# Skip term on TensorE, a third yy buffer, row sums in their own PSUM tile, and a table of the task order

## The chip, the core and the metric

One core of a Trainium2 chip runs the whole program. It has five engines, each with its own queue that runs in order: TensorE (matmul; "PE", with weight loads "PEld"), VectorE ("DVE"), ScalarE ("ACT"), GpSimd ("POOL") and SyncE ("SP", which issues most DMAs). Engines wait for each other through semaphores. The metric is the device time of one execution in microseconds (us). The runs before lie between 969.08 and 975.69 us.

## The reference

One layer with adaptive layer norm: a state-space convolution (S4D) and a gated feed-forward part, on a sequence of 2048 rows of 640 channels.

```python
dt = exp(log_dt); A = -exp(log_A_real) + 1j * A_imag
C = (C_real + 1j * C_imag) * dt[:, None]
P = exp((A * dt[:, None])[:, :, None] * pos)         # 640 x 128 x 2048
K = 2 * einsum("dn,dnl->dl", C, P).real
y = irfft(rfft(u.T, 4096) * rfft(K, 4096), 4096)[:, :2048].T + u * D_skip
mod = silu(c) @ w_mod                                 # sa, ca, ga, sb, cb, gb
x = x + ga * y(layernorm(x) * (1 + ca) + sa)
h = layernorm(x) * (1 + cb) + sb
x = x + gb * ((silu(h @ w1) * (h @ w3)) @ w2)
```

The skip term u * D_skip is the same as D_skip added to the element of K at lag zero.

## The kernel before

The 640 channels run as five blocks (b = 0 to 4) of 128. For each block the kernel does, on a mixture of all engines:

- **Generation** (tasks g{b}.{c}, eight chunks c of 16 channels; function gen_chunk). GpSimd adds up phases (ph) and multiplies exponent tables into sizes (z0 to z2: two into the tile yy, one into xx). ScalarE turns phases into sines and cosines (s0 to s4, PSUM tiles tr). VectorE multiplies sizes and sines (m0 to m4), in place in yy and xx. TensorE multiplies yy and xx (task p, 32 instructions in four column groups) into a PSUM tile kps of 128x256: values of the kernel K. ScalarE copies it to the tile ks (task r), and VectorE adds D_skip (tile dsk) to column 63 of each of the four rows of 64, which is lag zero (task d).
- **Normalised input** (tasks h{b}.{i}): rows of x are loaded (tile xq), normalised by ScalarE or VectorE into a PSUM tile hn (n; four instructions), multiplied and shifted by VectorE (x, a; tile hb), stored to DRAM and fetched in another order into the tile xb.
- **First transform** (hh{b}.{i} of xb and k{b}.{i} of ks): TensorE into PSUM tiles ps, copied by ScalarE or VectorE into sp or sp2.
- **Second transform, product, inverse** (w{b}.{i} and z{b}.{j}): TensorE makes fh and fk, ScalarE copies fh to hz, VectorE multiplies them as complex numbers into fp, TensorE transforms back into fz, and ScalarE or VectorE copies fz to zt, which SP stores to the DRAM tensor zd.

The tables of exponents of a block come from al8{b} (al times 0 to 7), exp{b} (ScalarE) and mag{b}.

After the last block comes a passage: zd is loaded again (iz, and izb for the last block's columns), TensorE makes the last transform (iy, iyb), VectorE adds it to x and takes the statistics of the second layer norm, TensorE turns the rows (tp) and the feed-forward part begins (gu, then groups with X, c and acc). The function ffn and what it calls run to the end.

The order up to the start of the feed-forward groups is not written out by hand. Every piece of work is a task with an engine (or a choice of two, as ("ACT", "DVE")), a duration that the code supposes, the tasks before it, and the buffers that it takes and gives back (rings: ph, xx, yy two each, kg two halves of kps, tr three, and so on). The planner, Plan.place, plays these durations through: it starts ready tasks by the rank of each, for which a list RANKS holds one number per task, and picks the engine that ends first where there is a choice. The kernel then emits the instructions in that order. As every engine runs its queue in order, this order decides what waits.

Most instructions go through one helper, so that all of them carry its line (157); the tiles tell them apart.

Of the kernel before, what the change touches and what calls it, by code (L numbers as in the profile page):

```python
# [29 lines left out]
EXPS = ((0, 0, 0, 64.0), (0, 1, 0, 1.0), (1, 0, 0, 512.0), (1, 1, 4, 8.0), (1, 2, 0, 8.0))  # L30
# [3 lines left out]
RANKS = """  # L34
# [65 lines left out]
"""  # L100
FP = 2
EPS = 1e-5
MAGIC = 1.5 * 2.0 ** 23
REV = float(2 ** 32 - 256)
# [63 lines left out]
class Plan:  # L168
# [101 lines left out]
    def run(self):  # L270
# [6 lines left out]
        for s, f, e, n in self.order:  # L277
            if T[n][2]:
                T[n][2](e)
# [1896 lines left out]
```

## Time and profile before

| | us |
|---|---|
| median of 3 runs | 973.34 |
| lowest, highest | 969.08, 975.69 |
| the profiled execution | 972.31 |
| its span, first to last instruction | 970.5 |
| TensorE busy in it | 859.9 |
| VectorE busy | 702.0 |
| ScalarE busy | 546.4 |
| GpSimd busy | 340.5 |

The time of an execution is a little longer than its span, by 1.8 us in the profiled one. Busy time is a sum over the whole span, in which the engine that limits changes, so shares of the whole say little; the stretches tell more. TensorE's granted clock was 0.975 of full speed over the span. In rows of the profile a group is named by tile written <- tiles read, without buffer numbers; the times of a group are its busy total, the mean of one instruction, and the idle time of its engine just before them with what ended it. Matmuls that the program issues once show as two records.

### The profile page before, as it was taken

The page shows a single profiled execution, that of the slowest core. Times are in us where ns is not written, and L with a number is a line of the kernel's source. Part 1 is how long each engine was busy: PE and PEld are TensorE (multiplying, and loading weights), DVE is VectorE, ACT ScalarE, POOL GpSimd, SP SyncE. Part 2 cuts the span into 40 slices and gives each one's busy share as a digit, 9 for nine tenths or more (in the row PEclk, how much of TensorE's full clock was granted, in tenths as well). Part 3 has the DMA queues.
Part 4 walks back from the last instruction along what each step waited for, and adds up shares of the span by engine and source line. Part 5 has one row for each costly group of instructions (what it writes and reads, how often), then busy time and mean ns, then how long its engine had stood idle before and what let it go on. Part 6 is the DMA issues. An engine that isn't in the chain of part 4 may idle for free.

```text
span 970.5 us, 20551 instructions
## 1 busy us (share of the span) xinstructions
PE 859.9 (89%) x7985; PEld 681.8 (70%) x7985; DVE 702.0 (72%) x1395; ACT 546.4 (56%) x1022; POOL 340.5 (35%) x371
## 2 busy tenths in 40 slices
PE   1464787889899997899999999999999999999997
PEld 1132665767778884677777778888788888888775
DVE  7998899999999968886767677557456464645422
ACT  6877788979888851564434455346444344443412
POOL 1797889879799600002111111000011212120000
PEclk9996999999999999799999999999999999999999
DMA  9955453723425268935434422276342322220374
GB/s 218 275 168 191 111 136 95 177 66 106 111 80 152 74 159 206 241 118 182 122 120 139 122 96 68 82 209 194 112 134 64 102 77 86 82 82 28 108 220 133
DMA packets 110506, 127.31 MB, mean 131 GB/s; under 512 B 10568, under 2 KB 90696, under 8 KB 109128
## 3 DMA queue, kind: packets, MB, share of 16 engines
q1 hardware_dynamic: 109032, 125.21, 45.3%
q8 instruction: 63, 1.03, 0.5%
q10 hardware_dynamic: 1376, 0.79, 0.3%
q14 instruction: 35, 0.29, 0.1%
HBM read 95.82 MB, written 30.15 MB: 130 GB/s over the span
## 4 chain that ended last, share of the span: by engine, by line
PE 70%; DVE 17%; ACT 5%; issue 4%; DMA 3%; POOL 1%; SPq 1%; ACTq 0%; DVEq 0%
PE c L157 19%; PE acc L157 18%; PE X L157 12%; PE ps L157 4%; PE gu L157 3%; DVE yy L157 3%; PE kps L157 3%; PE fz L157 2%; PE fk L157 2%; DVE fp L157 2%; PE fh L157 2%; DVE hn L157 2%; DVE xx L157 2%; DVE xb L157 1%; ACT tr L157 1%
## 5 line engine op out<-in xcount | busy, mean ns | idle before, releaser
L157 PE MATMUL acc<-ah,w 128*128 128x512 f32 x560 | 173.2, 395 | 2.4 <-DMA w<-w2d 1.7
L157 PEld LDWEIGHTS acc<-ah,w 128*128 128x128 f32 x560 | 103.7, 188 | 26.4 <-issue 2.1
L157 PE MATMUL acc<-al,w 128*128 128x512 f32 x260 | 102.4, 394 | 0.0
L665 DVE TENSOR_TENSOR wl<-s,wh 128x256 fp32r<-128x256 f32 x92 | 38.9, 423 | 67.5 <-ACT wh L664 67.1
L841 POOL TENSOR_TENSOR s<-wr 128x256 f32<-128x256 f32 x22 | 16.4, 744 | 187.8 <-DMA wr<-in_w 94.8
L157 POOL TENSOR_TENSOR ph<-p,p 128x1024 int32<-128x1024 int32 x40 | 79.2, 1979 | 8.2 <-ACT tr L157 8.0
L664 ACT ACTIVATE wh<-s 128x256 fp32r<-128x256 f32 x92 | 37.6, 410 | 78.5 <-PE X L157 58.1
L157 PE MATMUL kps<-yy,xx 128*32 128x64 f32 x2560 | 51.8, 234 | 28.6 <-DVE xx L157 21.4
L157 DVE TENSOR_TENSOR yy<-yy,tr 128x512 f32<-128x512 f32 (+1 forms) x80 | 75.3, 943 | 1.2 <-ACT tr L157 0.6
L157 PEld LDWEIGHTS kps<-yy,xx 128*32 128x32 f32 x2560 | 45.1, 116 | 38.3 <-issue 22.0
L664 ACT ACTIVATE wh<-wr 128x256 fp32r<-128x256 f32 x92 | 38.4, 418 | 56.0 <-PE X L157 42.3
L842 POOL TENSOR_TENSOR s<-s,wr 128x256 f32<-128x256 f32 x22 | 16.6, 755 | 134.0 <-issue 133.9
L902 ACT ACTIVATE t<-g 128x512 f32<-128x512 f32 x44 | 27.8, 632 | 52.7 <-DVE g L866 52.7
L157 ACT ACTIVATE tr<-ph,hpi 128x512 f32<-128x512 f32 x80 | 54.6, 690 | 4.4 <-DVE xx L157 2.7
L157 PEld LDWEIGHTS acc<-al,w 128*128 128x128 f32 x260 | 48.9, 188 | 10.8 <-DVE al L665 0.3
L871 DVE SCALAR_TENSOR_TENSOR g<-t,g 128x512 f32<-128x512 f32 x48 | 33.7, 702 | 31.3 <-ACT t L902 29.3
L157 POOL TENSOR_TENSOR yy<-e,e 128x512 f32<-128x512 f32 x48 | 52.4, 1109 | 8.8 <-PE kps L157 5.9
L157 DVE TENSOR_TENSOR xx<-tr,xx 128x512 f32<-128x512 f32 x80 | 54.3, 680 | 1.1 <-ACT tr L157 1.1
L157 PE MATMUL ps<-wk,ks 128*64 128x128 f32 x640 | 42.4, 285 | 13.6 <-DVE ks L157 8.9
L157 ACT ACTIVATE tr<-ph 128x512 f32<-128x512 int32 x80 | 47.3, 598 | 12.4 <-DVE yy L157 6.5
L157 PE MATMUL ps<-wk,xb 128*64 128x128 f32 x640 | 46.1, 295 | 6.3 <-ACT sp L157 3.0
L157 PEld LDWEIGHTS ps<-wk,ks 128*64 128x64 f32 x640 | 37.0, 143 | 20.3 <-ACT hn L157 6.6
(448 smaller groups left out, 2379.7 us busy)
## 6 DMA issues: line engine op xcount, KB each, us to landing
w<-w2d SPq DMA_DIRECT2D x42, 640.0 KB, 3.9
wr<-in_w SPq DMA_DIRECT2D x50, 320.0 KB, 3.9
zd<-zt SPq DMA_DIRECT2D x40, 256.0 KB, 2.9
w2d<-w SPq DMA_DIRECT2D x14, 640.0 KB, 3.5
xs<-in_x SPq DMA_DIRECT2D x16, 320.0 KB, 11.3
hs<-hb SPq DMA_DIRECT2D x20, 256.0 KB, 2.5
xb<-hs SPq DMA_DIRECT2D x20, 256.0 KB, 4.9
iz<-zd SPq DMA_DIRECT2D x32, 160.0 KB, 5.0
```

What stands on the lines that cost most here:

```text
L157: self.prev = self.k.order(f(*a, **kw), self.prev)
L664: self.nc.scalar.activation(H, v, AF.Copy)
L665: eng.tensor_tensor(Lo, v, H.bitcast(F32), op=ALU.subtract)
L841: eng.tensor_tensor(s[0], u[:, 0:2], u[:, 2:4], op=ALU.add)
L842: eng.tensor_tensor(s[1], s[0], g[:, 0:2], op=ALU.subtract)
L871: V.scalar_tensor_tensor(g, th, 1.0, g, op0=ALU.add, op1=ALU.mult)
L902: tanh = lambda o, i: A.activation(o, i, AF.Tanh, scale=0.5)
```

## The change

Five things change, all in the part ahead of the feed-forward groups.

1. The skip term. The task d on VectorE is gone. Behind the 32 products of a chunk, TensorE adds D_skip into column 63 by four products of 32x32 with four columns (identity times dsk), on the four diagonal corners of the array.
2. Ten of the 40 chunks (every third one of the first four blocks) keep yy in memory that belongs to the tile x2[0], which is needed only later: a third buffer (ring yz).
3. kps is a tile of its own per chunk, with one buffer (ring kg has one instead of two halves). ScalarE's copy r gives it back.
4. The order. Plan.place and its numbers are gone; ORDER lists the index of every task in the order in which it is emitted, and a mark ' where the second engine of a choice is taken. Nothing is played through any more.
5. What the order stands on: al8 is made in the tile of the table itself, so that it needs no tile of its own (the exponents are then taken with the one that overwrites it last); the products x0 and x1 are one task; the first two tiles of iz lie in sp2 and so can be loaded before the generation buffers are closed; fh and fk have another order of their four parts. The code for other forms of the product (FORM) is there but every block uses the same as before.

The supposed durations of many tasks change as well, but nothing reads them now.

```diff
-        self.plan = plan = Plan(ph=2, xx=2, yy=2, tr=3, kg=2, f2=3, bank=4, hz=3, xq=2, fp=FP, zt=3, xs=4, st=1, gu=3, tmp=7, w2=3)
+        self.plan = plan = Plan(ph=2, xx=2, yy=2, yz=1, tr=3, kg=1, f2=3, bank=4, hz=3, xq=2, fp=FP, zt=3, xs=4, st=1, gu=3, tmp=7, w2=3)
...
-RANKS = """
--1152 -1540 -1534 -1515 -1509 -1417 -1345 -1436 -1412 -1402 -1385 -1330 -1273 -1351 -1452 -1478 -1480 -1475 -1459 -1510 -1507
+ORDER = """
+1 78 80 81 82 83 150' 84 2 19 20 21 22 23 14 15 41 42 43 24 25 16 44 45 46 47 26 17 27 48 36 49 18 50 4 37 5 51 96 33 30 28 100 98
...
-EXPS = ((0, 0, 0, 64.0), (0, 1, 0, 1.0), (1, 0, 0, 512.0), (1, 1, 4, 8.0), (1, 2, 0, 8.0))
+EXPS = ((0, 0, 0, 64.0), (1, 0, 0, 512.0), (1, 1, 4, 8.0), (1, 2, 0, 8.0), (0, 1, 0, 1.0))
...
+    def in_third(self, b, c):
+        return b < NB - 1 and (8 * b + c) % 3 == 2
+
+    def third(self):
+        return self.x2[0].rearrange("p j d -> p (j d)")[:, :2048].rearrange("p (r d a i) -> p r d a i", r=2, d=self.CD, a=2)
...
-        yy = w.tile([P, 2, C, 2, 32], F32, name=f"yy_{d0}", tag="yy")
+        yy = self.third() if self.in_third(d0 // P, d0 % P // C) else w.tile([P, 2, C, 2, 32], F32, name=f"yy_{d0}", tag="yy")
...
+            for q in range(4):
+                g = slice(32 * q, 32 * q + 32)
+                nc.tensor.matmul(kps.rearrange("p (e b) -> p e b", b=64)[g, :, 63], self.ident[g, g], self.dsk[g, d0 // P, d0 % P // 4:d0 % P // 4 + 4],
+                                 start=False, stop=True, skip_group_check=True, tile_position=(32 * q, 32 * q))
...
-                if b == c == 0:
-                    self.kg = self.psg.tile([P, 2, 256], F32, name="kps", tag="kg", bufs=1)
-                kps[c] = self.kg[:, c % 2]
+                kps[c] = self.psg.tile([P, 256], F32, name=f"kps{b}{c}", tag="kg", bufs=1)
...
-        def skip(c):
-            o = slice(4 * c, 4 * c + 4)
-            V.tensor_add(self.ks[b][:, o, 63], kps.pop(c).rearrange("p (e b) -> p e b", b=64)[:, :, 63], self.dsk[:, b, o])
...
-            add(n + "d", "DVE", .1, lambda c=c: skip(c), [n + "r"] + (["dsk"] if b == 0 else []), t + 3, give=[("kg", n + "p")])
...
-        four = lambda x: x.rearrange("p (q r d) -> p q r d", q=2, r=2)
+        four = lambda x: x.rearrange("p (r q d) -> p q r d", q=2, r=2)
...
-            if u < 3:
-                z[u] = [self.ip.tile([P, 2, 512], F32, name=f"iz{u}{pr}", tag=f"iz{pr}", bufs=3) for pr in range(2)]
-            else:
-                z[u] = [self.xb[:, 1024 * pr:1024 * pr + 1024].rearrange("p (a d) -> p a d", a=2) for pr in range(2)]
+            s = self.sp2.rearrange("p a b c -> p (a b c)")
+            t = s[:, :2048] if u == 0 else s[:, 2048:] if u == 1 else self.xb if u == 3 else self.ip.tile([P, 2048], F32, name="iz2")
+            z[u] = [t[:, 1024 * pr:1024 * pr + 1024].rearrange("p (a d) -> p a d", a=2) for pr in range(2)]
...
+    def sequence(self):
...
+        for x in ORDER.split():
+            n = names[int(x.rstrip("'"))]
...
+            out.append((engs[x.endswith("'")], n))
```

Three places show how the instructions move. The first is VectorE's queue in the second block, at the chunks that start with channels 224 and 240 (the number behind tr); ks<-kps,dsk is the skip addition, hn<-xq the normalising. Before:

```order
L157 TENSOR_TENSOR yy_1627<-yy_1627,tr_224_1848 128x1024
L157 TENSOR_TENSOR ks_1194<-kps,dsk 128x4
L157 TENSOR_SCALAR hn<-xq_1590,rs_y_h,rs_n_h 128x128 x4
L157 TENSOR_TENSOR fp_1828<-fk_1859,hz_1854 128x2x2x128
L157 TENSOR_TENSOR xx_1626<-tr_224_1868,xx_1626 128x512
L157 TENSOR_TENSOR fk_1859<-fk_1859,hz_1854 128x512
L157 TENSOR_TENSOR hn<-hn,rw 128x512
L157 TENSOR_TENSOR fp_1828<-fp_1828,fk_1859 128x256 x2
L157 TENSOR_TENSOR hb_1958<-hn,rw 128x512
L157 TENSOR_TENSOR ks_1194<-kps,dsk 128x4
L157 TENSOR_SCALAR hn<-xq_1703,rs_y_h,rs_n_h 128x128 x4
L157 TENSOR_TENSOR xx_1697<-tr_240_1870,xx_1697 128x512
```

The same chunks after the change, where x_94 is the third yy buffer:

```order
L151 TENSOR_TENSOR xx_1721<-tr_224_1820,xx_1721 128x512
L151 TENSOR_TENSOR hn<-hn,rw 128x512
L151 TENSOR_TENSOR hb_1894<-hn,rw 128x512
L151 TENSOR_TENSOR x_94<-x_94,tr_224_1919 128x1024
L151 SCALAR_TENSOR_TENSOR yy_1853<-yy_1853,tr_240_1923 128x16x32
L151 TENSOR_TENSOR yy_1853<-yy_1853,tr_240_1923 128x16x32
L151 TENSOR_TENSOR xx_1721<-tr_224_1938,xx_1721 128x512
L151 COPY sp<-ps_1979 128x64x8
L151 TENSOR_TENSOR hn<-hn,rw 128x512
L151 TENSOR_TENSOR hb_1995<-hn,rw 128x512
L151 COPY sp_1013<-ps_2006 128x64x8
L151 COPY sp<-ps_2015 128x64x8
```

The skip additions are gone and the normalising has left VectorE (over the kernel 20 of these instructions stay on it instead of 44), while copies of ps have come to it (27 instead of 20).

The second place is TensorE's queue at the first second-transform groups (fh, fk) of block 0, between two chunks of generation. Before:

```order
L157 MATMUL kps<-yy_1091,xx_1090 32x64 x32
L157 MATMUL fh_1341<-sp,wb 64x128 x8
L157 MATMUL fk_1354<-sp,wb 64x128 x8
L157 MATMUL fh_1372<-sp,wb 64x128 x8
L157 MATMUL fk_1392<-sp,wb 64x128 x8
L157 MATMUL kps<-yy_1171,xx_1170 32x64 x32
```

After:

```order
L151 MATMUL kps_1342<-yy_1137,xx_1136 32x64 x32
L151 MATMUL kps_1342<-dsk,ident 32x4 x4
L151 MATMUL fh_1395<-sp,wb 64x128 x8
L151 MATMUL fh_1412<-sp,wb 64x128 x8
L151 MATMUL fk_1433<-sp,wb 64x128 x8
L151 MATMUL fk_1456<-sp,wb 64x128 x8
L151 MATMUL kps_1465<-yy_1191,xx_1190 32x64 x32
L151 MATMUL kps_1465<-dsk,ident 32x4 x4
```

Each chunk has four skip products behind its own 32; between two chunks other groups stand as before.

The third place is SP's queue at the end of the last block: xb<-zd loads the fourth inverse tile, zd<-zt stores a result of the last block, izb<-zd loads its columns. Before:

```order
L157 DMA xb<-zd 64x2x512 x4
L157 DMA zd<-zt_5189 128x4x128
L157 DMA zd<-zt_5191 128x4x128
L157 DMA zd<-zt_5208 128x4x128
L157 DMA zd<-zt_5210 128x4x128
L157 DMA izb_5243<-zd 64x4x128 x2
```

After:

```order
L151 DMA xb<-zd 64x2x512 x2
L151 DMA zd<-zt_5316 128x4x128
L151 DMA zd<-zt_5332 128x4x128
L151 DMA zd<-zt_5337 128x4x128
L151 DMA xb<-zd 64x2x512 x2
L151 DMA izb_5402<-zd 64x4x128 x2
```

Two of the four loads of the inverse tile have moved behind the last stores.

More of the change, by code (lines that the diff above doesn't have):

```diff
@@ L168 @@
 class Plan:
-    LAG = dict(PE=0.2, DVE=0.18, ACT=0.2, POOL=0.15, SP=0.0)
-    CHAIN = dict(DVE=0.12, ACT=0.12, POOL=0.07)
-    NEAR, RATE, LAND, FLY, ISSUE, AWAY, TABLE = 0.1, 235e3, 1.3, 0.7, 0.06, 8, 1.28
     def __init__(self, **rings):
@@ L258, in place @@
+        taken, done, out = {r: [] for r in self.n}, set(), []
+        for x in ORDER.split():
+            n = names[int(x.rstrip("'"))]
+            engs, _, _, after, _, _, take, give, _, _ = T[n]
+            assert n not in done and done.issuperset(after), n
+            for r, y, _ in take:
+                i = len(taken[r]) - self.n[r]
+                assert i < 0 or not uses[r, taken[r][i]], n
+                taken[r].append(y)
             for k in give:
                 uses[k] -= 1
-                given[k] = max(fin + self.LAG.get(e, 0.0), given.get(k, 0.0))
@@ L261, in place @@
[L261 to L279 removed]
+            done.add(n)
@@ L282 @@
+            out.append((engs[x.endswith("'")], n))
+        assert len(done) == len(T)
+        return out
+    def run(self):
+        for e, n in self.sequence():
+            if self.tasks[n][2]:
+                self.tasks[n][2](e)
 class K:
@@ L1113, in dst @@
                         return z[u][pr][h * 64:h * 64 + 64]
-                    load(f"iz{u}.{pr}{h}", zv[:, t0:t0 + 2, :cut], dst, 262144, done + ([f"hh{b4}.{i}.m" for i in range(8)] if u > 2 else []))
+                    load(f"iz{u}.{pr}{h}", zv[:, t0:t0 + 2, :cut], dst, 262144, done + ([f"hh{b4}.{i}.m" for i in range(8)] if u > 2 else []),
+                         "inv" if u < 2 else "change")
         def load_up(m):
@@ L1135, in load_down @@
                      [f"w2l{0 if m == 1 else 13}"] if m in (1, 2) else [])
[L1137 removed]
+        used = [f"g{b4 - 1}.{c}.z{i}" for c in (5, 6, 7) for i in range(3)] + [f"mag{b4 - 1}", f"exp{b4 - 1}"]
         for b, src in ((0, b4 - 1), (1, b4)):
@@ L1613, in border @@
             self.x2 += [self.fp.tile([P, 4, D], F32, name=f"x2{i}") for i in (2, 3)]
-        plan.add("change", None, 0, change, [f"g{b}.7.p", f"g{b}.7.d"] + [f"h{b}.{i}.x" for i in range(4)], 0, own=True)
+        plan.add("change", None, 0, change, [f"g{b}.7.p", f"g{b}.7.r"] + [f"h{b}.{i}.x" for i in range(4)], 0, own=True)
         self.tail_tasks(border, cut)
```

269 lines of the change are left out of this document (117 added, 152 removed), and 87 rows, old and new, of tables (ORDER, RANKS).

## The prediction

> **What bounds the kernel now.** I first cut the span into stretches of busy time, at the points where the chain of waits changes its character. The columns are the stretch, its length, busy time (and instructions) of TensorE, its weight loads, VectorE, ScalarE and GpSimd, then the granted clock, the DMA share and GB/s.
>
> ```profile
> core 0: us, PE busy (x) PEld busy (x) DVE busy (x) ACT busy (x) POOL busy (x), PEclk, DMA share, GB/s
> 0.00:100.00 100.00, 41.52 (x633) 23.90 (x633) 87.83 (x171) 75.12 (x143) 66.43 (x80) 0.90 0.74 210
> 100.00:252.00 152.00, 124.75 (x2464) 103.80 (x2464) 145.42 (x275) 128.95 (x217) 132.20 (x132) 0.96 0.49 124
> 252.00:376.00 124.00, 118.93 (x2312) 98.26 (x2314) 109.62 (x208) 86.49 (x156) 75.45 (x72) 1.00 0.44 116
> 376.00:398.00 22.00, 13.92 (x79) 8.87 (x76) 19.45 (x76) 6.47 (x10) 0.63 (x1) 0.72 0.91 215
> 398.00:441.00 43.00, 41.00 (x184) 32.75 (x183) 35.78 (x68) 25.78 (x46) 0.91 (x1) 0.99 0.59 176
> 441.00:971.00 530.00, 519.77 (x2319) 414.21 (x2317) 303.95 (x601) 223.60 (x453) 64.91 (x87) 1.00 0.38 115
> ```
>
> From 441 us on TensorE is busy 519.77 of 530 us, in code that the change leaves alone. Whatever the change does must be done before that. There VectorE is the full engine from 100 to 252 us (145.42 of 152), and TensorE from 252 to 376 us (118.93 of 124). The chain of waits says the same; its columns are start, length, engine, tile and line:
>
> ```profile
> 251.81 0.61 DVE xx L157
> 252.55 0.87 PE kps L157 x41
> ...
> 373.19 2.01 PE fz L157 x8
> ...
> 376.30 3.14 DMA zd<-zt
> ...
> 380.31 4.67 DMA izb<-zd
> ...
> 398.07 8.88 PE gu L157 x36
> ```
>
> Up to 252 us the chain runs mostly over VectorE pieces, then over TensorE up to the last inverse product at 373 us, then over two transfers into the first feed-forward product at 398 us. So the sum has three parts: VectorE's work before 252 us, TensorE's work from 252 to 376 us, and the passage to 398 us.
>
> **The change part by part.** These groups carry the prices (busy total and mean ns behind the first bar, idle time before them behind the second):
>
> ```profile
> L157 DVE TENSOR_TENSOR ks<-kps,dsk 128x4 f32<-128x4 f32 x40 | 6.0, 157 | 9.8 <-ACT ks L157 5.6 <-PE kps L157 3.1 <-ACT hn L157 1.1
> L157 DVE TENSOR_SCALAR hn<-xq,rs_y_h,rs_n_h 128x128 f32<-128x128 f32 x44 | 18.1, 412 | 1.2
> L157 DVE COPY sp<-ps 128x512 f32<-128x512 f32 x20 | 13.4, 683 | 3.2 <-PE ps L157 3.1
> L157 DVE TENSOR_TENSOR xs_al<-al,j 128x1024 f32<-128x1024 f32 x1 | 2.8, 2835 | 0.0
> L157 DVE TENSOR_TENSOR late<-late,mag 128x512 f32<-128x512 f32 x1 | 1.7, 1718 | 0.0
> L157 DVE TENSOR_SCALAR p<-pB 128x128 int32<-128x128 int32 x4 | 1.9, 481 | 0.0
> L157 ACT ACTIVATE hn<-xq,rs_n_h,rs_y_h 128x128 f32<-128x128 f32 x20 | 9.2, 462 | 2.5 <-DMA xq<-in_x 1.7 <-DVE fp L157 0.3
> L157 ACT ACT_TABLE_LOAD x12 | 15.4, 1283 | 1.3 <-PEq L2172 0.7 <-DVE xx L157 0.4
> L157 ACT ACTIVATE sp<-ps 128x512 f32<-128x512 f32 x60 | 35.3, 595 | 11.0 <-PE ps L157 10.0 <-DMA xs_w<-in_w_mod 0.7
> ```
>
> *The skip additions on VectorE go.* All 40 of 157 ns go; by the stretches 24 of them, 3.58 us, lie before 252 us:
>
> ```profile
> 0.00:100.00 100.00, 0.79 (x5) 0.30 (x1) 0.90 0.74 210
> 100.00:252.00 152.00, 2.79 (x19) 0.00 (x0) 0.96 0.49 124
> ```
>
> They also held VectorE's queue for 9.8 us, because each waited in order for ScalarE's copy of its chunk. Of that the list of VectorE's waits from 252 us on has 5.8 us, where VectorE doesn't bind:
>
> ```profile
> DVE ks L157 <- ACT ks L157: 5.0, 4, 2.8
> ...
> DVE ks L157 <- PE kps L157: 0.8, 1, 0.8
> ```
>
> That leaves 4.0 us before 252 us. Part of it comes back at the next instruction, which may be no readier: between 0 and 4.0 I take 2.0.
>
> *The order moves work off VectorE.* Counted over the two programs, 24 of the 44 normalising instructions go to ScalarE (24 x 412 ns = 9.9 us); the exponent and magnitude products of the second block, done beside busy GpSimd, go to GpSimd (2.84 + 1.72); two p copies go too (2 x 481 = 0.96). The hn row stands the same in the list for 100 to 252 us alone, and the two products stand in the chain before:
>
> ```profile
> 88.58 2.76 DVE xs_al L157
> ...
> 98.62 1.72 DVE late L157
> ```
>
> Seven more copies of sp come to VectorE (683 ns each), of which the first three blocks have a net three: +2.0 us.
>
> Before 252 us: -3.6 - 2.0 - 9.9 - 4.6 - 1.0 + 2.0 = **-19.1 us**.
>
> Is there cover for it on the others? TensorE has 124.75 us of work in 152, and keeps its skip products (below, 18 chunks x 0.3 = 5.4): 130.2 us in a stretch that by VectorE shrinks by some 12 to 140, a load of 93%, where it reached 96% from 252 us on. GpSimd gets two products more, in the first 100 us where it idles 33.6. ScalarE is the narrow one: see the second rival.
>
> *The skip products on TensorE come.* Four 32x32 products with four columns per chunk, so 40 x 4 instructions. No row shows one. Nearest below is the chunk's own product, 32 instructions in 64 records, 1.10 us; nearest above the four small products of the modulation, 8 records in a row, 1.05 us:
>
> ```profile
> 317.36 0.91 PE fh L157 x16
> 318.27 1.10 PE kps L157 x61
> ...
> 321.29 1.06 PE fk L157 x16
> ...
> 103.50 1.05 PE L157 MATMUL pv<-ident,mc 128*128 128x4 f32 x8
> 252.00:376.00 124.00, 18.47 (x960) 15.79 (x960) 2.45 (x16) 6.11 (x16) 1.00 0.44 116
> ```
>
> At 1.10/64 a record, 8 records are 0.14 us; serial they would be 1.05. A group that follows one of another shape also shows 1.06 where the same sixteen take 0.91: 0.15 for the change of shape. I take 0.14 + 0.15 = 0.3 us, near the lower end since the four lie in four corners of the array as the chunk's own do. From 252 us on 960/64 = 15 chunks pay it on the engine that binds: **+4.5 us** (+2.1 to +15.8). Before that it is covered as shown above. The Trainium skill, TensorEngine Tiling (Array Packing), section Instruction Overhead, says that a product of one column takes as long as one of 60; this would set each of the four at the price of the chunk's own 64-column products, and the sum by it would be 2.1 instead of 4.5, the lower end.
>
> *Third yy buffer, single kps tile.* GpSimd waited 14.9 us for the two yy buffers:
>
> ```profile
> POOL yy L157 <- PE kps L157: 14.9, 11, 3.9
> ```
>
> GpSimd isn't on the chain there, so I count nothing for it. The row sums now have one PSUM tile where two halves rotated: the next chunk's product waits in TensorE's queue until ScalarE has copied the last one, and everything behind it waits too. In the new order at least one other group of 0.9 us or more stands between two chunks, which covers a copy of 0.38 us (15.06 us over 40); if ScalarE is late the wait shows. Zero, with the rivals for more.
>
> *The passage.* On SP the last two loads of the fourth inverse tile now stand behind the stores of the last block, in front of the loads of the last columns:
>
> ```profile
> iz<-zd SPq DMA_DIRECT2D x32, 160.0 KB, 5.0
> 386.61 0.69 DVE L157 TENSOR_TENSOR x<-iyb,x 128x512 f32<-128x512 f32 x1 [1.33 <-PE iyb L157]
> ```
>
> Issued near 376.7 us, where the store's piece of the chain starts, they land some 5 us later; two row products, two additions of 0.69 us and statistics stand before the addition that now starts at 386.61. I estimate 387.4 in its place: **+0.8 us** (0 to 1.5). The feed-forward part gets the same instructions: 0.
>
> Sum: -19.1 + 4.5 + 0.8 = -13.8 us. The profiled run was 972.31 us (span 970.5), so 958.5 there; the median of the runs, 973.34, lies 1.0 above it: **960 us** rounded up. Own range: waits 2.0 either way, skip products -2.4 to +4, passage 0.8: 953 to 967.
>
> **The rivals.**
>
> *ScalarE takes over (964 to 972, say 966).* From 100 to 252 us ScalarE has 128.95 us of work; 24 x 462 ns and one table load come, two copies of 595 go: 128.95 + 11.1 + 1.3 - 1.2 = 140.2 us, which is the whole 140 that VectorE would leave. At VectorE's present density of 145.42/152 it needs 146.5, so 6.5 of the gain goes: -7.3 in all. Against it: ScalarE idles 24.9 us in the first 100 and 37.5 from 252 us on, and an order can move work there.
>
> *The four products run one after another (980).* This is the slower end. At 1.05 us a chunk, 15 chunks cost 15.8 in the bound stretch, and before it TensorE has 124.75 + 18.9 = 143.7 us, at 96% density 149.6 instead of 140: -13.8 + 11.3 + 9.6 = +7, 979.4 for the profiled run. It decides from about 0.8 us a chunk. For it: the pv row. Against: the chunk's own products overlap. It is also what a rule would do: the Trainium skill, TensorEngine Tiling (Array Packing), section Restrictions and Gotchas, says that different row tiles cannot use the same PSUM bank at once, and these four are row tiles with one target tile; no row before shows row tiles on one bank.
>
> *The order packs better (948).* All 4.0 us of waits go, the skip products cost 2.1, and the 6.6 us that VectorE idles between 100 and 252 us go to work: 958.5 - 2.0 - 2.4 - 6.6 + 1 = 948.5. For it: GpSimd runs ahead with the third buffer. Against: every engine is over 80% there.
>
> **How the numbers follow.** Forecast 0.57, ScalarE 0.22, serial products 0.10, better packing 0.11. Less than about 1% (963.6 to 983.1 around 973.34) can't be told from no change. Faster: 0.57 x 0.85 + 0.22 x 0.2 + 0.11 = 0.64. Same: 0.57 x 0.15 + 0.22 x 0.8 = 0.26. Slower: the serial case, 0.10, counted whole although its 980 lies just inside 1%, since the price leaves out what queues behind TensorE. The range 947 to 975 holds the first, second and fourth case.
>
> **What would show it.** The additions ks<-kps,dsk are gone; VectorE's busy total up to the last inverse product falls by some 17 us; hn on ScalarE stands at 44 and TensorE is under 97% before the handover. Chunk groups of kps rise from 1.10 to some 1.4 us: 2 or more proves the serial rival. The last fz should start near 360 instead of 373, and the first gu near 385. ScalarE at 95% or more before the handover, with VectorE waiting for tr, would make the second rival right. Waits of kps for ScalarE's ks would show the single tile, which I count as free.

## The result, and the profile after

| | before | after |
|---|---|---|
| median of 11 runs each, us | 974.80 | 968.31 |
| lowest to highest | 969.08 to 976.63 | 965.61 to 969.84 |
| ratio, 95% interval | | 0.9944, 0.9926 to 0.9962 |
| the profiled execution, its span | 972.31, 970.5 | 969.31, 967.5 |
| VectorE, ScalarE busy in it | 702.0, 546.4 | 697.6, 554.9 |

The change gains 5.4 us by the ratio (3.7 to 7.2 by its interval), where 13 were forecast. The direction is right, and more than half of the gain is missing: 968.3 lies above the forecast's own range of 953 to 967, and inside 947 to 975 only because that takes the rivals in.

The same stretches as before, with the same columns (stretch, length, busy time of TensorE, its weight loads, VectorE, ScalarE, GpSimd, then granted clock, DMA share, GB/s), of the changed kernel:

```profile
0.00:100.00 100.00, 37.16 (x532) 21.07 (x533) 87.46 (x166) 73.92 (x139) 63.18 (x80) 0.88 0.77 204
100.00:252.00 152.00, 132.07 (x2835) 111.84 (x2825) 137.96 (x232) 137.41 (x241) 133.53 (x132) 0.96 0.42 113
252.00:376.00 124.00, 118.27 (x2388) 96.17 (x2386) 110.01 (x193) 88.16 (x155) 78.15 (x75) 1.00 0.50 131
376.00:398.00 22.00, 15.10 (x79) 9.65 (x76) 19.75 (x69) 5.34 (x9) 0.63 (x1) 0.77 1.04 245
```

From 100 to 252 us VectorE fell from 145.42 to 137.96 and ScalarE rose from 128.95 to 137.41: two engines at 90% where one stood at 96%. Most of what VectorE no longer does there did not become time; VectorE idles instead. The groups say on whom it waits (busy total and mean ns, then the idle time before them and what ended it):

```profile
L151 DVE TENSOR_TENSOR xx<-tr,xx 128x512 f32<-128x512 f32 x80 | 54.4, 683 | 8.1 <-ACT tr L151 7.8
L151 DVE TENSOR_SCALAR hn<-xq,rs_y_h,rs_n_h 128x128 f32<-128x128 f32 x20 | 8.2, 412 | 0.8 <-ACT zt L151 0.2
L151 DVE COPY sp<-ps 128x512 f32<-128x512 f32 x27 | 18.0, 683 | 1.3 <-PE ps L151 1.2
L151 ACT ACTIVATE hn<-xq,rs_n_h,rs_y_h 128x128 f32<-128x128 f32 x44 | 20.4, 464 | 1.1
L151 PE MATMUL kps<-dsk,ident 32*32 32x4 f32 x320 | 9.8, 181 | 0.0
```

In the kernel before, the first of these waited 1.1 us for ScalarE's tr; now 7.8. Where the stages stand, in us from the start of the span:

| | before | after | difference |
|---|---|---|---|
| ScalarE's copy of the last chunk's row sums | 346.44 | 344.48 | -2.0 |
| first fh of the last block | 349.87 | 346.14 | -3.7 |
| last fz | 373.19 | 371.57 | -1.6 |
| first gu | 397.73 | 396.13 | -1.6 |
| end of the span | 970.5 | 967.5 | -3.0 |

This execution was a late one: four of the experiments below (e2, e7, e13, e15) have the same instructions up to the last chunk, and copied its sums at 341.6 to 342.2. Measured by those, some 4.5 us are gained there, against the one profile of the kernel before, which is 2.5 us below that kernel's median; so this is good to some 2 us. About 1 is lost on the way to gu (51.3 us from that copy before, 52.3 in e13), and 1.4 come behind it (572.8 us from gu to the end, then 571.4).

The loss in the last block has one place. TensorE's rows (start, length, group, idle time before it and what ended it), and the pieces of the chain that lead there:

```profile
361.58 1.08 PE L151 MATMUL fh<-sp,wb 128*64 128x128 f32 x16
365.30 1.14 PE L151 MATMUL fh<-sp,wb 128*64 128x128 f32 x16 [2.63 <-ACT zt L151]
```

```profile
342.56 6.06 DMA sp<-zd
...
351.04 7.46 DMA sp<-zd
...
360.09 4.45 DMA zd<-zt
...
364.64 0.61 ACT zt L151
```

sp<-zd are loads of the first two tiles of iz, which lie in sp2; the new order puts them ahead of the stores on SP. SP waited for two of them to land; the store zd<-zt therefore went out at 360.09, its buffer came free at 364.5, ScalarE copied into it, and TensorE had idled 2.63 us.

### The profile page after: what moved, and what is told of

The parts are those of the page before. It is cut to its first block, busy times and chain, and to the rows that moved or that the text cites. A ratio compares the mean times of both kernels' runs of the same rounds, so it can differ in the third digit from the quotient of the medians.

```text
span 967.5 us, 21165 instructions
## 1 busy us (share of the span) xinstructions
PE 861.4 (89%) x8305; PEld 684.7 (71%) x8305; DVE 697.6 (72%) x1334; ACT 554.9 (57%) x1041; POOL 342.1 (35%) x375
## 3 DMA queue, kind: packets, MB, share of 16 engines
q8 instruction: 65, 1.06, 0.5%
## 4 chain that ended last, share of the span: by engine, by line
PE 66%; DVE 8%; ACT 6%; DMA 4%; issue 3%; SPq 1%; POOL 0%; DVEq 0%; ACTq 0%
PE c L151 19%; PE acc L151 18%; PE X L151 12%; PE ps L151 3%; PE gu L151 3%; PE kps L151 2%; PE fh L151 2%; PE fz L151 2%; PE fk L151 2%; DMA sp<-zd 1%; PE iy L151 1%; DVE fp L151 1%; DVE yy L151 1%; ACT tr L151 1%; DVE hn L151 1%
## 5 line engine op out<-in xcount | busy, mean ns | idle before, releaser
L151 DVE TENSOR_TENSOR yy<-yy,tr 128x512 f32<-128x512 f32 (+1 forms) x60 | 56.7, 946 | 4.5 <-ACT tr L151 2.8
L805 DVE SCALAR_TENSOR_TENSOR g<-t,g 128x512 f32<-128x512 f32 x48 | 33.7, 702 | 31.5 <-ACT t L836 29.6
L599 DVE TENSOR_TENSOR wl<-wr,wh 128x256 fp32r<-128x256 f32 x92 | 40.3, 438 | 15.0 <-ACT wh L598 14.9
L151 PE MATMUL kps<-yy,xx 128*32 128x64 f32 x1920 | 38.2, 234 | 14.1 <-DVE xx L151 11.5
L151 PEld LDWEIGHTS kps<-yy,xx 128*32 128x32 f32 x1920 | 33.5, 116 | 23.2 <-issue 13.0
L151 PE MATMUL fz<-fp,wz 64*128 64x512 f32 x160 | 43.0, 627 | 5.9 <-DVE fp L151 4.6
```

The source lines that it names most:

```text
L151: self.prev = self.k.order(f(*a, **kw), self.prev)
L599: eng.tensor_tensor(Lo, v, H.bitcast(F32), op=ALU.subtract)
L805: V.scalar_tensor_tensor(g, th, 1.0, g, op0=ALU.add, op1=ALU.mult)
```

## The experiments

Each was run in five rounds beside the kernel before on the same chip; ratios are to that. A difference from the changed kernel is worked out from the ratio, 0.001 being 0.97 us; with intervals of about 0.0015 to 0.0025 either way, under 2 us can't be told from none. "Last chunk" is ScalarE's copy of the last chunk's row sums. In the table of the order a number is a task, a mark ' the second engine of its choice.

### One part undone, or done alone

**e1: the normalising back on VectorE**, at the same places.

```diff
-554 564 817 827 1080 1085
+554' 564' 817' 827' 1080' 1085'
```

> The changed kernel, with the 24 normalising instructions of the second to fourth block back on VectorE at the same places of the order. Theory A (ScalarE became as full as VectorE between 100 and 252 us, 137.4 and 138.0 us busy, so the 9.9 us that VectorE lost were not a gain): VectorE goes to about 148 us and ScalarE to about 126 there, the time stays within 2 us of the changed kernel's 968.3. Rival B (VectorE is the bound as the forecast counted it, and what is missing of the gain was lost elsewhere): the 9.9 us come back in full, about 978.

Ratio 1.0022 (1.0005 to 1.0038): 7.6 us worse than the changed kernel, nearer to rival B. Read beside the next run, it is not the worth of the move.

**e5: the same 24 instructions to ScalarE, in the kernel before**, nothing else.

```diff
         for s, f, e, n in self.order:
             if T[n][2]:
-                T[n][2](e)
+                T[n][2]("ACT" if n in ("h1.0.n", "h1.2.n", "h2.1.n", "h2.3.n", "h3.2.n", "h3.3.n") else e)
```

> The kernel before, in its own order, with the same 24 normalising instructions on ScalarE that the change moves there, and nothing else. Theory A (the forecast's term: VectorE is the bound between 100 and 252 us and ScalarE has room): 9.9 us less than before, a ratio of 0.990. Rival B (what putting them back in the changed kernel cost, 7.6 us, is their worth): 0.992. Rival C (ScalarE has no room in an order made without them, and the chunks wait for its sines): no gain, 0.997 to 1.003.

Ratio 1.0060 (1.0048 to 1.0072): 5.8 us *slower*. VectorE's waits between 90 and 200 us (engine and tile that waited, on whom; total, times, longest):

```profile
DVE hn L157 <- ACT hn L157: 10.4, 4, 4.5
DVE sp L157 <- PE ps L157: 3.0, 1, 3.0
DVE hn L157 <- ACT sp L157: 2.6, 1, 2.6
```

Before, the first of these stood at 0.6. VectorE's next step multiplies hn, so what it no longer computes it waits for, behind whatever stands in ScalarE's queue. Both orders lose 6 to 8 us when these six tasks change engine and nothing else does, whichever way they go. So neither run gives a worth of the instructions that holds without the order. None of the three theories held in full; A fell.

**e4: the skip term alone, in the kernel before.** The four products go behind each chunk as in the change, and the additions are taken out:

```diff
-            V.tensor_add(self.ks[b][:, o, 63], kps.pop(c).rearrange("p (e b) -> p e b", b=64)[:, :, 63], self.dsk[:, b, o])
+            kps.pop(c)
```

> The kernel before, in its own order, with only the skip term moved: VectorE's 40 additions are gone and TensorE has the four products behind each chunk. Theory A (the step's own terms with the measured 0.17 us: 3.6 us of additions and 2.0 of waits less on VectorE, 2.6 more on TensorE): 3.0 us less than before, 971.8. Rival B (with the forecast's 0.3 us): 1.1 less, 973.7. Rival C (the waits of the additions come back in full at the next instruction and the additions were slack): 1 to 3 more, 975.8 to 977.8.

Ratio 0.9999 (0.9978 to 1.0020). A's 3.0 less is outside the interval (2.1 less to 2.0 more), B's 1.1 less and the lower end of C inside. The skip term's move alone is worth nothing that can be measured, although VectorE's busy time up to the last chunk fell by 4.4 us (319.6 to 315.2).

**e3: the changed kernel without the skip products.**

```diff
-            for q in range(4):
-                g = slice(32 * q, 32 * q + 32)
-                nc.tensor.matmul(kps.rearrange("p (e b) -> p e b", b=64)[g, :, 63], self.ident[g, g], ...
```

> The changed kernel without the four skip products of each chunk: D_skip is left out of the result. Theory A (a group costs the 0.17 us that its start to the next start shows, on the 15 chunks of the stretch where TensorE binds): 2.6 us less, 965.7. Rival B (0.3 us as the forecast had it, with the change of shape): 4.5 us less, 963.8. Rival C (TensorE no longer binds before the feed-forward part, other engines do): under 1 us, 967.5 to 968.3.

Ratio 0.9931 (0.9905 to 0.9956), 1.3 us less. Rival B's 4.5 lies just outside what the two intervals allow (1.3 +- 3); A and C can't be told apart. The rows of the changed kernel give the price of one group directly:

```profile
330.11 0.24 PE L151 MATMUL kps<-dsk,ident 32*32 32x4 f32 x8
330.28 1.13 PE L151 MATMUL fz<-fp,wz 64*128 64x512 f32 x4
```

From its start to the next group's start are 0.17 us, for four products; 33 of the 40 groups show the same.

**e6: the exponent and magnitude products of the second block back on VectorE.**

```diff
-408 410
+408' 410'
```

> The changed kernel, with the exponent and the magnitude product of the second block back on VectorE, as before. Theory A (the forecast's term: 4.6 us of VectorE's time were saved and were worth as much): 4.6 us more than the changed kernel, a ratio to before of 0.999. Rival B (VectorE has as much busy time in the first 100 us as before, 87.5 against 87.8 us, because its small instructions there grew longer beside GpSimd, 0.7 to 2.7 us for h_nm, 0.7 to 2.4 for the first magnitude product; the term was paid back): within 1.5 us of the changed kernel, 0.993 to 0.996.

Ratio 0.9952 (0.9938 to 0.9965), 0.8 us more: the 4.6 of the term are not there. But B's mechanism fell with it. In e6 the two products take 2.07 and 0.95 us, and the small instructions stay as long as in the changed kernel. Those of the changed kernel, and in the second fence GpSimd beside them:

```profile
35.55 2.43 DVE L151 TENSOR_TENSOR e<-e,mag 128x512 f32<-128x512 f32 x1
37.90 1.91 DVE L151 TENSOR_SCALAR h_nm<-h_nm 128x4 f32<-128x4 f32 x1
```

```profile
35.15 4.63 POOL L151 TENSOR_TENSOR ph<-p,p 128x1024 int32<-128x1024 int32 x2
```

An instruction on 128x4 elements took 1.91 us: it ended at 39.81, when GpSimd's second ph ended (39.78). In the kernel before, the same two took 0.68 and 0.16 us, at 31.5 to 32.3, in a gap of GpSimd's. So the new order, not the move of the two products, put them beside it. The Trainium skill, SBUF — State Buffer, section "SBUF: two separate sides", says that VectorE (in a two-port mode, or reading two inputs from SBUF) and GpSimd take a shared pair of ports for a whole instruction, and that the other waits it out. The first row, with two inputs, agrees in its length; for the second, with one input, the trace shows only the wait until GpSimd's end, not which of these conditions it meets.

**e8: two halves for the row sums.**

```diff
-                kps[c] = self.psg.tile([P, 256], F32, name=f"kps{b}{c}", tag="kg", bufs=1)
+                if b == c == 0:
+                    self.kg = self.psg.tile([P, 2, 256], F32, name="kps", tag="kg", bufs=1)
+                kps[c] = self.kg[:, c % 2]
```

> The changed kernel, with the row sums of a chunk in two halves of one PSUM tile again, taken in turn; the order stays. Theory A (the forecast: the single tile costs nothing, since other groups cover ScalarE's copy): within 1 us of the changed kernel, a ratio to before of 0.9935 to 0.9955. Rival B (TensorE waits for the copy of ks and what is queued behind it waits too): 2 to 3 us less, 0.991 to 0.9925.

Ratio 0.9950 (0.9935 to 0.9965), 0.6 us more, that is none. A holds: the single tile costs nothing that can be measured.

### What a microsecond costs on either engine

e1 and e5 change what waits for what. So work was added that nothing waits for: 24 instructions of a constant 128x128 tile into a spare one, behind the six normalising groups (VectorE's form, shown here, in e9 and e11; ScalarE's in e10 and e14).

```diff
-        c.tile([P, 32], F32, name="pad")
+        self.dummy = c.tile([P, P], F32, name="spare")
...
+        if (pc, b) in ((1, 0), (1, 2), (2, 1), (2, 3), (3, 2), (3, 3)):
+            for j in range(4):
+                self.nc.vector.tensor_scalar(self.dummy, self.ident, rstd[:, 0:1], nb[:, 0:1], op0=ALU.mult, op1=ALU.add)
```

e9, in the changed kernel, on VectorE:

> The changed kernel with 24 additional instructions on VectorE that nothing waits for, of the form of the normalising ones (a constant 128x128 tile into a spare tile), at the places in the order of the six normalising groups that went to ScalarE: about 24 x 0.44 = 10.6 us more of VectorE's time and no other change. Theory A (VectorE still sets the pace between 100 and 252 us, as the forecast assumed for its gain): 9 to 10.6 us more, a ratio to before of 1.0035 to 1.0055. Theory B (VectorE, 90.8% busy there, now waits for ScalarE and TensorE and has room for a part): 4 to 7 more, 0.9985 to 1.0015. Rival C (ScalarE alone is the bound): under 2 more, below 0.9965.

e10, in the changed kernel, on ScalarE:

> The changed kernel with 24 additional instructions on ScalarE that nothing waits for, of the form of the normalising ones, at the same six places: about 24 x 0.46 = 11.1 us more of ScalarE's time and no other change. If ScalarE sets the pace together with VectorE (90.4% busy between 100 and 252 us, theory B): 6 to 11 us more, a ratio to before of 1.0005 to 1.0055. If VectorE alone sets it (theory A): under 3 more, below 0.9975.

e11 and e14, in the kernel before, on VectorE and on ScalarE:

> The kernel before, in its own order, with the same 24 additional instructions on VectorE behind its own. Theory A (VectorE is the bound there, 95.7% busy between 100 and 252 us, so a microsecond of its work is a microsecond of the kernel): 9 to 10.6 us more, a ratio of 1.009 to 1.011. Rival (VectorE's neighbours bind as well, and it has room): under 6, below 1.006.

> The kernel before, in its own order, with the 24 additional instructions of e10 on ScalarE. Read at the copy of the last chunk's row sums, since the feed-forward part is longer by the spare tile. Theory A (ScalarE has room in the order before, so it became a second bound by the change): of the 11.8 us added under 5 show there, where VectorE's 16.5 in e11 showed as 17.3. Theory B (in the order before, too, ScalarE's sines are waited for): 8 to 11 show.

The ratios are 1.0161, 1.0158, 1.0254 and 1.0168, with intervals of 0.002 to 0.003 either way, far above every ratio expected. Of each, 8 to 9 us stand behind the first gu, where none of these instructions is, and e13 is for that: only the spare tile.

```diff
-        c.tile([P, 32], F32, name="pad")
+        c.tile([P, P], F32, name="pad")
```

> The changed kernel with nothing but an unused tile of the first pool widened from 32 to 128 columns, as the spare tile of e9 to e11 did, which moves the later tiles of on-chip memory by 384 bytes. Theory A (the 8 us that e9 to e11 show behind the first feed-forward product, 579.5 to 581.0 against 571.4 us, come from where the tiles lie): 8 us more than the changed kernel, all behind gu; the copy of the last chunk's row sums stays near 344.5 us; a ratio to before of 1.002 to 1.0035. Rival (the additional instructions did it): as the changed kernel, 0.993 to 0.996.

Ratio 1.0046 (1.0030 to 1.0061). Theory A holds: the last chunk is copied at 342.02, as ever, and from gu to the end pass 580.1 us instead of 571.4. So e9 and e10 are read against e13, and e11 and e14 at the last chunk. The added instructions took, in e9, e10, e11 and e14 in turn:

```profile
L151 DVE TENSOR_SCALAR spare<-ident,rs_y_h,rs_n_h 128x128 f32<-128x128 f32 x24 | 14.4, 599 | 0.7
```

```profile
L151 ACT ACTIVATE spare<-ident,rs_n_h,rs_y_h 128x128 f32<-128x128 f32 x24 | 11.8, 490 | 0.6
```

```profile
L157 DVE TENSOR_SCALAR spare<-ident,rs_y_h,rs_n_h 128x128 f32<-128x128 f32 x24 | 16.5, 689 | 0.7
```

```profile
L157 ACT ACTIVATE spare<-ident,rs_n_h,rs_y_h 128x128 f32<-128x128 f32 x24 | 11.8, 493 | 0.6
```

| | added, us | cost, us | per us |
|---|---|---|---|
| after, VectorE (e9 less e13) | 14.4 | 11.2 | 0.78 |
| after, ScalarE (e10 less e13) | 11.8 | 10.9 | 0.92 |
| before, VectorE (e11, last chunk 363.92 less 346.44) | 16.5 | 17.5 | 1.06 |
| before, ScalarE (e14, last chunk 355.28 less 346.44) | 11.8 | 8.8 | 0.75 |

A profiled execution is good to some 2 us and the intervals to 3, so these prices are good to some 0.2; read at the last chunk too, e9 and e10 give 0.86 and 1.07. By them e9 is nearer to theory A, e11 has its theory A (and more than its 9 to 10.6 us), and e10 and e14 have their theories B: at these six places work added to VectorE or to ScalarE sets the pace, in both kernels. A microsecond given to ScalarE costs nearly as much as one on VectorE, and in the kernel before already 0.75. The profile before showed ScalarE 85% busy from 100 to 252 us, and the forecast had read that as room. No such price was measured for TensorE.

Does taking away work with the same prices? In e17 and e18 each of the six groups is one instruction of 128x512 instead of four, on ScalarE in the changed kernel, on VectorE in the one before.

```diff
+            if (pc, b) in ((1, 0), (1, 2), (2, 1), (2, 3), (3, 2), (3, 3)):
+                if j == 0 and e == "DVE":
+                    self.nc.vector.tensor_scalar(out, x, rstd[:, s], nb[:, s], op0=ALU.mult, op1=ALU.add)
+                elif j == 0:
+                    self.nc.scalar.activation(out, x, AF.Identity, scale=rstd[:, s], bias=nb[:, s])
-            if e == "DVE":
+            elif e == "DVE":
```

> The changed kernel; each of the six normalising groups that went to ScalarE is one instruction of 128x512 instead of four of 128x128, which takes the mean and scale of the group's first rows for all of them, so that part of the normalisation is left out of the result. ScalarE has 24 x 0.464 - 6 x 0.60 = 7.5 us less, and nothing else changes. Theory B (what ScalarE got counts on the path, 10.2 of 11.8 us in e10): 5 to 6.5 us less than the changed kernel at the last chunk and in all, a ratio to before of 0.988 to 0.9895. Rival A (VectorE alone sets the pace and e10's cost was one of a longer queue only): under 2, 0.9925 to 0.9945.

> The kernel before; the same six groups, on VectorE there, each as one instruction of 128x512 with the first rows' mean and scale, so that part of the normalisation is left out of the result. VectorE has 24 x 0.44 - 6 x 0.68 = 6.5 us less and ScalarE nothing more: the forecast's term with ScalarE's share taken off. Theory B (VectorE's time alone is worth about what it says, 17.5 of 16.5 us in e11, and the change lost it because the same work then stood on ScalarE): 5 to 7 us less than before at the last chunk and in all, a ratio of 0.993 to 0.995. Rival C (a shorter VectorE only waits longer for the sines, whoever normalises): under 2, 0.998 or more.

The six took 4.7 us on ScalarE (777 ns each) and 4.8 on VectorE (807), so 6.4 and 5.1 were taken away. e17: 0.9928 (0.9907 to 0.9950), 1.6 us less than the changed kernel, 0.25 per us, not to be told from none. e18: 0.9963 (0.9944 to 0.9982), 3.6 less than before, 0.7 per us; its twelve runs spread from 965.98 to 972.69, and the profiled one, among the longest, gains 0.9 us at the last chunk (345.54). So freeing VectorE *without* loading ScalarE does pay by the ratio, somewhere under its price (between B and C). Freeing ScalarE pays far less than loading it costs: e17's number is rival A's, although e10 speaks against A's reason.

With the prices of the table, e1 and e5 can be read again, as an estimate. In e1, 9.9 us more on VectorE at 0.78 are 7.7, and 7.6 were measured, so the 11.2 us taken off ScalarE gave back nothing. In e5, 11.2 us more on ScalarE at 0.75 are 8.4, and 5.8 were measured, so the 9.9 us taken off VectorE gave back little. e4 and e17 say the same. As I read them together, in an order that stays as it is, added work is paid nearly in full, while what is taken off one full engine is soon stopped by the next. That reading was not tried further, and e18's ratio fits it only in part.

### Taking the new waits away

**e2: the stores of the last block directly behind their copies**, in SP's queue (the eight moved alike; two shown).

```diff
-1391' 1473 1477 1393' ... 1392 ... 1394
+1391' 1392 1473 1477 1393' 1394
```

> The changed kernel, with the eight stores of the last block's inverse products moved in SP's queue directly behind the copies that they wait for, ahead of the loads of the last transform that stood in front of them. Theory A (a store that waited behind loads on SP kept ScalarE's next copy 3.0 us from its buffer and TensorE idle for 2.6 us at 362.7): the 2.6 us gap in front of the last fh goes and the time falls by 1.5 to 3, to 965.3 to 966.8. Rival B (the end of the passage is set by when the loads land): the gap goes, the loads land later by as much, and the time stays at 968.3 or rises by up to 2.

Ratio 1.0023 (1.0006 to 1.0040), 7.7 us worse; the 2.6 us gap went, as both theories said, and a larger one came:

```profile
368.37 3.79 PE L151 MATMUL fz<-fp,wz 64*128 64x512 f32 x8 [5.16 <-ACT hz L151]
```

A weight load behind the stores was now late, and a weight split that waited for it stood ahead of hz on ScalarE.

**e7: six of the stores from ScalarE's queue** instead (the order also moves a weight split and two loads, as its expectation says).

```diff
-            nc.sync.dma_start(o.rearrange("q r t d -> (r t) q d"), held.pop(("z", j, f)))
+            (nc.scalar if b == NB - 1 and j < 3 else nc.sync).dma_start(o.rearrange("q r t d -> (r t) q d"), held.pop(("z", j, f)))
```

> The changed kernel, with six of the eight stores of the last block issued from ScalarE's queue behind its copies, so that they neither wait behind SP's loads nor hold them, the last weight split of the second matrix behind the copies, and the last two loads of the fourth inverse tile ahead of the last two stores on SP. Theory A (the two queues cost the last block 2.6 us of idle TensorE, and e2 lost it again only because SP and a weight load then held others): the last fz starts some 2.5 us earlier after the block's first fh than the 25.4 us of the changed kernel, and the time falls by 2 to 3.5 us, a ratio to before of 0.991 to 0.992. Rival B (the end of the passage hangs on the loads' landing times): under 1 us, 0.9935 to 0.9945.

Ratio 1.0033 (1.0021 to 1.0045), 8.7 worse. ScalarE stood 12 us before its stores could go out, until earlier loads had landed, and its copies stood behind them:

```profile
361.50 1.22 ACTq L151 DMA_DIRECT2D zd<-zt  x2
362.81 1.09 ACT L151 ACTIVATE hz<-fh 128x512 f32<-128x512 f32 x2 [12.33 <-DMA iz<-zd]
```

**e15: four stores first, the other four behind the loads, the weight split behind the copies.**

```diff
-1391' 1473 1477 1393' ... 1392 ... 1394 1485 1431 1426
+1391' 1392 1473 1477 1393' 1394 ... 1431 1426 1485
```

> The changed kernel, with the first four stores of the last block directly behind their copies on SP, the other four behind the remaining loads of the last transform, and one weight split of ScalarE's queue (the one that waited for its load in e2) behind the copies of the block. Theory A (the idle 2.6 us in front of the last block's fifth pair of products is a wait of the queues alone): last fz 22.8 us behind the block's first fh instead of 25.4, 1 to 3 us less than the changed kernel, a ratio to before of 0.9915 to 0.9935. Rival B (the sixteen loads and eight stores of that stretch are limited by the transfers themselves): the wait turns up at another load, 0.994 or more.

Ratio 0.9961 (0.9948 to 0.9974), 1.7 us worse. The block does what A says: its last fz is 22.5 us behind its first fh instead of 25.4. Then the passage gives it back; the rows of the last transform now read

```profile
374.71 2.82 PE L151 MATMUL iy<-xb,late 128*64 128x512 f32 x8 [0.23 <-PE iy L151]
381.12 0.40 PE L151 MATMUL iyb<-izb,late 128*64 128x128 f32 x2 [3.59 <-DMA izb<-zd]
383.97 1.94 PE L151 MATMUL iyb<-izb,late 128*64 128x128 f32 x14 [2.44 <-DMA izb<-zd]
```

and gu starts 53.3 us behind the first fh, where it was 50.0 (47.9 before the change). This is rival B's sign: the wait turned up at another load. The loads izb<-zd waited until the last store had landed at 377.46, 5.5 us after it was issued; in the changed kernel the last store took 3.4. As the DMA engines are 90% busy or more from 350 to 376 us, I take that stretch to be bound by its transfers; a ScalarE copy that still waited 5.4 us behind a weight split (366.9 us) may have its part.

**e12: three pieces of ScalarE's sines ahead of two copies** that waited for TensorE at 98.5 us (granted clock 0.54 from 101.0 to 104.7 us).

```diff
-283 262 333 288 284 335 277 149 0 417 282 281 290 289 285 340 286
+283 284 285 286 262 333 288 335 277 149 0 417 282 281 290 289 340
```

> The changed kernel with three pieces of ScalarE's work on the last chunk of the first block (a sine, the magnitudes of the phases and a cosine) moved in front of two copies that wait there for TensorE, at 98.5 to 104.7 us: VectorE waited 5.1 us for the first of them. Theory A (VectorE sets the pace, and what it idles is lost): the wait goes and the time falls by 3 to 5 us, a ratio to before of 0.989 to 0.9915. Theory B (what VectorE does next waits for TensorE, whose clock is granted at 0.73 to 0.93 there, so the idle time moves to the next wait): under 1.5 us, 0.993 to 0.996.

Ratio 0.9929 (0.9905 to 0.9953), 1.5 us less, not to be told from the changed kernel. The wait of 5.14 us became three:

```profile
102.43 0.69 DVE L151 TENSOR_TENSOR xx<-tr,xx 128x512 f32<-128x512 f32 x1 [1.98 <-POOL xx L151]
103.46 2.01 DVE L151 TENSOR_TENSOR yy<-yy,tr 128x512 f32<-128x512 f32 x2 [0.33 <-POOL yy L151]
107.81 0.69 DVE L151 TENSOR_TENSOR xx<-tr,xx 128x512 f32<-128x512 f32 x1 [2.34 <-ACT tr L151]
```

That is theory B in kind, with GpSimd and ScalarE where I expected TensorE.

**e16: e12 and e15 together**, by both of their diffs.

> The edits of e12 and e15 together. Theory A (both waits were lost time): the sum of the two, 2 to 4 us less than the changed kernel, a ratio to before of 0.990 to 0.9925. Rival B: not below the better of the two alone.

Ratio 0.9959 (0.9947 to 0.9972): rival B. Of the full computation, e12 has the lowest median (966.90), but no run beat the changed kernel by more than the measurement resolves.

## Where the prediction was right, and where it failed

**The bound.** Right, and too simple. VectorE was an engine that bound before 252 us (1.06 per us added). That ScalarE at 85% was slack was not right: e14. Whether TensorE at 82% was slack, no run shows.

**The step that failed** is "Before 252 us: -3.6 - 2.0 - 9.9 - 4.6 - 1.0 + 2.0 = -19.1 us", taken as time: up to the last chunk the kernel gained 2.0 us in the profiled execution and some 4.5 in the four others. Two things are wrong in the step.

*Its size.* Summed by rows up to the last chunk, VectorE's instructions fell from 358.9 to 348.3 us, by 10.6. The forecast's own rows (without the 2.0 of waits, with all 39 additions that stand there) make 19.5. The term of the copies was mis-sized: eight more of sp by then, +5.5 and not +2.0, as I had netted them over blocks. Not foreseen at all were one more copy of zt (0.7) and the growth of pieces that stayed, most of it beside GpSimd, by a net 4.7. And the skip addition's 157 ns is not what it holds VectorE for:

```profile
195.27 0.15 DVE L157 TENSOR_TENSOR ks<-kps,dsk 128x4 f32<-128x4 f32 x1
195.34 0.69 DVE L157 TENSOR_TENSOR fk<-fk,hz 128x512 f32<-128x512 f32 x1
```

The next starts 0.07 us behind it, as behind most of the others: 24 of them are 1.7 us and not 3.6. Busy time without overlap fell by only 5.2 us (319.6 to 314.5), and idle time rose by 3.2.

*Its worth.* The largest term, 24 x 412 ns, was set against nothing, although the list gave ScalarE 24 x 462 for it; the forecast left that to a rival. By the prices above, as an estimate, -9.9 x (0.78 to 1.06) + 11.2 x (0.75 to 0.92) is between -2 and +3: the exchange would be worth about nothing. Over the whole stretch, -10.6 on VectorE and the +9.8 by which ScalarE's rows grew up to the last chunk (309.1 to 318.8, with two table loads more, 2.6, where the rival had one) give -3.9 to +0.7; measured are 2.0 and some 4.5 less, the second just outside. This estimate uses prices of added work, and e17 and e18 paid less for work taken away. So it is shown that ScalarE's share had to be charged, and not how the two shares add up.

*The direction* came out right in part by luck: the sum that gave it rests on a term for which no run shows a gain that holds without the order, and what made the 4.5 us is open. The signs that the forecast named for its gain failed with it: the last fz starts at 371.57 and not near 360, the first gu at 396.13 and not near 385.

**Skip products.** Mis-sized on the safe side: 0.3 us forecast, 0.17 measured, so 2.6 and not 4.5 for 15 chunks (a chunk's group with them takes 1.27 to 1.29 us in the chain, where the forecast named 1.4); leaving all out gave 1.3 (e3). The step as a whole, forecast at -1.1, measured at -0.1 +- 2 (e4).

**Third buffer and single tile at nothing.** The tile: right (e8). The buffer wasn't tried alone, since the order relies on it.

**The passage at +0.8.** From the last fz to gu, which that term is about, it took 24.5 us before and 24.6 after (25.5 in e13): within the 0 to 1.5 stated. What was not foreseen lies ahead of it. From the block's first fh to gu 2.1 us were lost (47.9 to 50.0), because the last stores waited behind earlier loads on SP. Counted from ScalarE's copy of the last row sums, gu comes only 0.3 us later (51.3 to 51.6), since the block began 1.7 us sooner behind it. e15 suggests that the transfers, not the order of two instructions, set the stretch.

**The rivals.** "ScalarE takes over" came nearest: 966 forecast for it, 968.3 measured, by its own signs (VectorE waiting for tr; ScalarE at 24.5 of 25 us from 150 to 175), if not at the 95% over the stretch that I had named. What it had wrong is "takes over": ScalarE shared the bound before already. The serial products fell: row tiles into one PSUM tile ran at 0.17 us for four, not 1.05, so nothing here shows the rule of the Trainium skill, TensorEngine Tiling (Array Packing), section Restrictions and Gotchas, as a cost in time. "Packs better" fell: VectorE's idle time grew.

**Open.** Why the feed-forward part is 1.4 us shorter after the change was not tried; e13 shows that the places of the tiles alone can do more. How the gain of some 4.5 us splits between the moved work and the order as a whole can't be had from runs that move one thing: e1, e2, e5 and e7 each cost 6 to 9 us, which I put down to an order made as a whole and then broken.

## What to carry to other kernels

When several engines stand at 80 to 95% in a stretch, work that is moved between them has two prices, and the engine that gets it must be charged about as much as the other is credited. Measure that price by adding instructions nobody waits for, on each engine. Expect less for work taken away: 0.25 and 0.7 per us here, both poorly resolved. In an order that was searched as a whole, an edit to one place can measure the broken order and not the edit, so read such a run only where undoing a move and doing it alone agree.

## What the runs showed of the hardware that was not expected

*Where the tiles lie.* An unused tile 384 bytes wider, and nothing else, made the feed-forward part 8.7 us longer (e13). No wait shows there: TensorE is busy throughout, at granted clock 1.00, but does 217 or 218 matmuls in 50 us instead of 220 or 221. The first fence is the changed kernel, the second e13, each in the first part of its feed-forward groups:

```profile
446.10:496.10 50.00, 50.00 (x221) 37.29 (x220) 34.78 (x77) 22.01 (x48) 8.89 (x12) 1.00 0.47 139
```

```profile
444.30:494.30 50.00, 50.00 (x217) 36.73 (x217) 34.17 (x75) 21.46 (x46) 8.96 (x12) 1.00 0.48 139
```

Why was not tried. Any experiment that adds a tile needs a run with the tile alone beside it.

*Small instructions beside GpSimd.* 128x4 elements on VectorE took 0.16 us at one place and 1.91 at another, until GpSimd's instruction ended.

*DMA issues wait for others.* A store on ScalarE's queue waited 12 us for a load that another queue had issued (e7), so a transfer's own queue does not tell what it waits for. The trace shows that the program ties them. Each transfer reports its landing by a semaphore, and the 422 transfers of this run share eight of them in turn. In front of the first store ScalarE's queue has a wait for the very semaphore that the store will use; its last user was a weight load that SP had issued at 355.80, which landed at 361.42, and the store went at 361.50. The second store waited so for a load of iz that landed at 362.27.
